# Value products scheduled in blocks of six pairs instead of single pairs, in a fused bucketed-attention and MLP kernel

## The chip, the cores and the metric

The kernel runs on one core of a Trainium2 chip. The metric is the device time of one execution in microseconds, as the median of several runs. Inside the core, TensorE (PE in the profile), VectorE (DVE), ScalarE (ACT) and GpSimd (POOL) work in parallel, each on its own queue of instructions in a fixed order; SyncE (SP) issues nearly all DMAs. An instruction that has to wait holds up everything behind it on its engine.

## What is computed

The reference is an attention layer in which a query sees only the keys of its own hash bucket, followed by a two-layer MLP with a squared ReLU. The sizes are 4 batches, 8 heads, 768 positions, head width 64, model width 512 and hidden width 2048:

```python
q_bits = (np.einsum('bhsd,dk->bhsk', q, proj) > 0)      # 6 bits, likewise k_bits
mask = q_bucket[:, :, :, None] == k_bucket[:, :, None, :]
scores = np.where(mask, scale * np.matmul(q, k.transpose(0, 1, 3, 2)), -1000000000.0)
attn = np.exp(scores - np.max(scores, axis=-1, keepdims=True))
attn = attn / (np.sum(attn, axis=-1, keepdims=True) + 1e-09)
x = np.matmul(attn, v)                                  # heads side by side: 3072 x 512
h = np.maximum(x @ w_in, 0.0)
out = h * h @ w_out
```

## The kernel before

**Work.** The attention is cut into 32 visits: a batch, a pair of heads and a half of the queries (384 of 768). A visit has six units, one for each head and each block of 128 queries. A unit (`unit`, line 669) multiplies queries and keys into the tile `pS` on PE, finds the row maximum `nmx` on DVE, takes the exponential `e` with its sum `sm` on ACT, and divides by the sum. In most visits the result is split into a high and a low float16 part, `hl`, which a DMA transposes into `aT`. In five early visits (`PLAIN_AV`, line 54) it stays float32 and PE transposes it through `pT`.

**Value products.** When the six units of a visit are done, `av` (line 707) multiplies `aT` by the values and accumulates in the PSUM tile `pA`. The two heads of the pair lie side by side: each matmul is 128 rows by 64 columns of TensorE, one head writes partitions 0 to 63 and the other 64 to 127, and the two of a pair run at the same time. A split visit takes 18 such pairs (six key chunks for each of high times high, low times high and high times low; values `VV`), a plain visit six pairs in float32 (values `V`). `xx`, the result in two float16 parts, is the input of the MLP.

**MLP.** When the four visits of a half batch are done, `moe` (line 726) computes the hidden layer into `pm` (384 columns in a matmul) and the output into `po` (512 columns), both with all 128 rows and columns of TensorE. There are eight such stages. They are the work that fills TensorE while softmax is under way; `pace` and `PACE` (lines 801 and 62) hold their matmuls back until given units have begun.

**What sets the order.** The functions do not issue instructions. They record operations in a `Program`, with their dependences and a rank. `order` (line 236) then plays the program through with assumed durations, backward for priorities and forward for an order on every engine, `ROUNDS` (4) times, and keeps the shortest plan. In `forward` (line 309) an engine that comes free takes the ready operation of the best priority. What it takes, it takes whole: an operation named `matmuls` holds a list of matmuls, which `emit` (line 392) issues one behind the other. Line 370 adds `SWITCH` (95 ns assumed) where an operation on PE uses another tiling than the one before it (`tiling`, line 219: rows and columns, so 128 by 64 for the value products, 128 by 128 for scores and MLP). The recorded order is issued as it stands, and nothing is reordered at run time.

Before the change each pair of value matmuls is one such operation:

```python
for n, (kc, d0, c) in enumerate(todo):
    matmuls(*[(pA[m], VV[:, h, kc, d0 : d0 + D], aTs[h][:, c]) for h, m in enumerate((T, U))],
            start=n == 0, stop=n == len(todo) - 1)
```

So between any two pairs of a visit the planner may put another operation: a score matmul, an MLP matmul, or a bucket matmul (`pc`).

Of the kernel before, what the change touches and what calls it, by code (L numbers as in the profile page):

```python
# [24 lines left out]
B, H, S, D = 4, 8, 768, 64  # L25
# [26 lines left out]
PLAIN, PLAIN_TO, ALTERNATE = 4, 8, 36  # L52

PLAIN_AV, DIVIDE = (0, 1, 2, 4, 5), ("pool",)

WHOLE = {0: 2}

# [373 lines left out]
def lsh_attention_moe(ctx: ExitStack, tc, kq, v, proj2, w_in, w_out, consts, out):  # L431
# [4 lines left out]
    pr = Program(tc)  # L436
    pe, dve, act, pool, sp = pr.pe, pr.dve, pr.act, pr.pool, pr.sp
    T, U = slice(0, D), slice(D, P)
# [6 lines left out]
    def move(out, x, scale=1.0, engines=(act, dve, pool)):  # L445
        ways = [(q, "tensor_scalar", (out, x, scale, 1.0, ALU.mult, ALU.mult), {}) for q in engines if q not in (act, sp)]
        if act in engines:
            ways.append((act, "activation", (out, x, AF.Identity if isinstance(scale, View) else AF.Copy), {"scale": scale}))
        if sp in engines:
            ways.append((sp, "dma_start", (out if out.dtype == x.dtype else out.bitcast(x.dtype), x), {}))  # L450
        pr.add(*ways)

    def left(out, x, scale, part):
        ways = [(dve, "scalar_tensor_tensor", (out, x, scale, part, ALU.mult, ALU.subtract), {})]
        if not isinstance(scale, View) and scale == 1.0:
            ways.append((pool, "tensor_tensor", (out, x, part, ALU.subtract), {}))
        pr.add(*ways)

    def sb(shape, dtype, name, bufs=1, tag=None):
        return pr.tile(sbp, "sb", shape, dtype, name, BUFS.get(tag or name, bufs), tag)  # L460

    def ps(shape, dtype, name, bufs=1, tag=None):
        return pr.tile(psp, "psum", shape, dtype, name, bufs, tag)
# [113 lines left out]
    def matmuls(*args, start=True, stop=True):  # L577
        pr.add((pe, "matmuls", [(a, {"start": start, "stop": stop}) for a in args], {}))
# [128 lines left out]
    def av(b, hp, half, VV, aTs):  # L707
        pA = ps([P, 512], F32, "pA")[:, 0:HS]
        plain = VV.dtype == F32
        todo = [(kc, t * D, kc + l * KC) for t, l in (((0, 0),) if plain else ((0, 0), (1, 0), (0, 1))) for kc in range(KC)]  # L710
        scale = vscales[b][0] if plain else 1.0 / ASC
        for n, (kc, d0, c) in enumerate(todo):
            matmuls(*[(pA[m], VV[:, h, kc, d0 : d0 + D], aTs[h][:, c]) for h, m in enumerate((T, U))], start=n == 0, stop=n == len(todo) - 1)
        xx = xxs[b, half, hp] = sb([P, 2, HS], F16, "xx")
        move(xx[:, 0], pA, scale)
        left(xx[:, 1], pA, scale, xx[:, 0])
# [117 lines left out]
    for n, (b, hp, half) in enumerate(visits):  # L834
        sts, aTs, plain = kept[b, hp], [], n in PLAIN_AV
        for h, st in enumerate(sts):
            aT = sb([P, KC, HS], F32, "aT") if plain else sb([P, 2 * KC, HS], F16, "aT")
            aTs.append(aT)
            for i in range(3):
                pr.rank = u  # L840
                unit(st, half, i, aT, plain)
                u += 1
        if n + 1 < len(visits):
            ready(*visits[n + 1][:2], u + PREP, n + 1 < PLAIN_TO and visits[n + 1][1] < PLAIN)
        if (b, hp, plain) not in kept_v or not alive([kept_v[b, hp, plain]]):
            pr.rank = u - 6 + PREP
            kept_v[b, hp, plain] = values(b, hp, plain)
        pr.rank = u - 0.5
        av(b, hp, half, kept_v[b, hp, plain], aTs)
        if n in early:  # L850
            do, j, pr.rank = early[n]
            do(j)
        done[b, half] = done.get((b, half), 0) + 1
        if done[b, half] == H // 2:
            moe(stages, b, half)
            stages += 1
# [35 lines left out]
```

## Time and profile before

| what | value |
|---|---|
| time, median of 3 runs | 905.26 us (904.71 to 906.72) |
| span of the profiled execution | 905.9 us |
| PE busy | 875.5 us, 97% |
| DVE busy | 614.0 us, 68% |
| ACT busy | 638.4 us, 70% |
| POOL busy | 108.5 us, 12% |
| mean granted TensorE clock | 0.998 |
| matmuls / weight loads recorded | 5090 / 5090 |

The span of 905.9 us runs from the first to the last instruction of the profiled execution; the page gives no other time for that execution, and the median of the timed runs lies 0.64 us below it. Busy time of PE is the union of the recorded matmuls, whose ends are modelled and overlap the next one's start. What a matmul takes from PE is therefore read from start to start, not from its recorded duration. In a timeline a row merges equal neighbours: its first two numbers are the start of the first and the time to the end of the last. All functions record through one helper, so nearly every row has the line L418 (L415 for a list of matmuls); the tile names tell the rows apart. A float32 matmul is recorded as two.

### The profile page before, as it was taken

Reading aid. Unit: us, or ns where it says so; the run is one execution under the profiler, and the core shown is the slowest. Engines: PE = TensorE matmul, PEld = TensorE weight load, DVE = VectorE, ACT = ScalarE, POOL = GpSimd, SP = SyncE. Lnnn points to the kernel's source line nnn. Section 1 sums busy time; section 2 is a strip of 40 time slices with the busy share of each in tenths; the row PEclk is TensorE's granted clock in tenths of the full one; section 3 lists DMA queues with packets and bytes.
Section 4 is the critical chain, followed back from the end, with each engine's and each line's share of the span. In section 5 each row is a group of like instructions: output and inputs, shape, how many; then the busy total and the mean of one; then the engine's idle time right before and its main releaser. Section 6 shows DMA issues by size and latency. Waiting matters only on the chain. (4 is left out here: it accounts for less than half of the span.)

```text
span 905.9 us, 14199 instructions
## 1 busy us (share of the span) xinstructions
PE 875.5 (97%) x5090; PEld 478.0 (53%) x5090; DVE 614.0 (68%) x1154; ACT 638.4 (70%) x1175; POOL 108.5 (12%) x159
## 2 busy tenths in 40 slices
PE   7998999999999999999999999999999999999997
PEld 5553544455555555555555555555555555544553
DVE  5899989978887778787776868886867651211111
ACT  3887676969797787888876877877767663432433
POOL 1665655100100000000000000000000000000000
PEclk9999999999999999999999999999999999999999
DMA  7548649978969797979897969896979452200000
GB/s 230 161 145 191 179 142 230 198 138 174 187 146 210 152 208 147 221 145 216 153 210 142 192 133 204 177 197 124 194 128 193 90 101 32 57 1 1 35 1 35
DMA packets 279974, 131.82 MB, mean 146 GB/s; under 512 B 258272, under 2 KB 258400, under 8 KB 279904
## 3 DMA queue, kind: packets, MB, share of 16 engines
q1 hardware_dynamic: 279424, 130.91, 68.9%
q8 instruction: 40, 0.66, 0.3%
q14 instruction: 30, 0.25, 0.1%
q10 hardware_dynamic: 480, 0.01, 0.0%
HBM read 37.30 MB, written 6.29 MB: 48 GB/s over the span
## 5 line engine op out<-in xcount | busy, mean ns | idle before, releaser
L418 PE MATMUL po<-wo,g 128*128 128x512 f16 x1152 | 334.3, 380 | 1.1 <-ACT o L418 0.8
L418 PE MATMUL pm<-xx,win 128*128 128x384 f16 x1536 | 322.6, 327 | 1.8 <-ACT xx L418 1.5
L418 DVE TENSOR_REDUCE nmx<-pS 128x1 f32<-128x768 f32 x192 | 182.9, 953 | 64.1 <-PE pS L418 61.2
L418 ACT ACTIVATE e<-pS,nmx 128x768 f32<-128x768 f32 x192 | 171.8, 895 | 70.1 <-DVE nmx L418 61.6
L418 PEld LDWEIGHTS <-win 128*128 128x128 f16 x1536 | 145.3, 98 | 114.7 <-issue 16.7
L418 DVE SCALAR_TENSOR_TENSOR hl<-e,rv,hl 128x768 f16<-128x768 f32 x162 | 164.0, 1013 | 20.9 <-ACT hl L418 20.5
L418 PEld LDWEIGHTS <-g 128*128 128x128 f16 x1152 | 107.2, 98 | 128.4 <-issue 26.4
L418 ACT ACTIVATE hl<-e,rv 128x768 f16<-128x768 f32 x156 | 144.5, 930 | 26.8 <-ACT e L418 18.3
L418 DVE SCALAR_TENSOR_TENSOR g<-g,g 128x384 f16<-128x384 f32 x123 | 68.4, 557 | 130.3 <-ACT g L418 129.3
L418 ACT ACTIVATE g<-pm 128x384 f32<-128x384 f32 x127 | 61.7, 486 | 106.5 <-PE pm L418 105.3
L418 ACT ACTIVATE g<-g 128x384 f32<-128x384 f32 (+1 forms) x252 | 130.8, 521 | 5.2 <-PE po L418 0.2
L415 PE MATMUL pA<-aT,VV 128*64 128x384 f16 x972 | 102.8, 332 | 0.0
L418 PE MATMUL pS<-A,Q 128*128 128x384 f32 x288 | 93.6, 405 | 5.9 <-ACT e L418 4.3
L418 POOL TENSOR_SCALAR rv<-sm 128x1 f32<-128x1 f32 x72 | 29.9, 415 | 528.1 <-ACT e L418 492.9
L418 PE MATMUL pS<-L,M 128*128 128x384 f32 x288 | 76.7, 346 | 2.5 <-DMA M<-Q 2.3
L415 PEld LDWEIGHTS <-VV 128*64 128x64 f16 x972 | 50.1, 109 | 50.4 <-issue 35.0
L418 PEld LDWEIGHTS pS<-A,Q 128*128 128x128 f32 x288 | 47.9, 189 | 34.5 <-ACT e L418 20.9
L418 PEld LDWEIGHTS pS<-L,M 128*128 128x128 f32 x288 | 51.4, 188 | 7.2 <-issue 3.5
L418 DVE TENSOR_SCALAR rv<-sm 128x1 f32<-128x1 f32 x120 | 18.2, 152 | 36.3 <-ACT e L418 33.1
L418 PE MATMUL pS<-A,L 128*128 128x384 f32 x96 | 38.4, 517 | 4.1 <-ACT e L418 3.6
L418 DVE TENSOR_SCALAR M<-pc,cst 128x384 fp32r<-128x384 f32 (+1 forms) x56 | 37.5, 670 | 1.8 <-PE pc L418 1.6
L418 PE MATMUL pS<-Q,M 128*128 128x384 f32 x96 | 37.3, 501 | 1.4 <-ACT e L418 1.4
(111 smaller groups left out, 671.1 us busy)
## 6 DMA issues: line engine op xcount, KB each, us to landing
R<-kq SPq DMA_DIRECT2D x24, 384.0 KB, 4.1
raw<-w_in SPq DMA_DIRECT2D x16, 511.8 KB, 3.5
raw<-w_out SPq DMA_DIRECT2D x16, 511.8 KB, 4.5
V<-vp SPq DMA_DIRECT2D x16, 384.0 KB, 4.9
out<-o SPq DMA_DIRECT2D x21, 256.0 KB, 3.5
Q<-L SPq DMA_DIRECT2D x24, 192.0 KB, 3.7
Q<-A SPq DMA_DIRECT2D x24, 192.0 KB, 3.1
A<-A SPq DMA_DIRECT2D x24, 192.0 KB, 3.5
```

The source lines that it names most:

```text
L415: ins = q.engine.matmul(*map(real, args), **kw).ins
L418: ins = getattr(q.engine, o.name)(*map(real, o.args), **{k: real(x) for k, x in o.kw.items()}).ins
```

## The change

`av` collects the matmuls of the pairs in a list and hands the list over after every sixth pair. A split visit becomes three operations of six pairs (twelve matmuls) instead of 18 of one pair, and a plain visit one operation of six pairs instead of six. The matmuls themselves, their operands and their order within the visit are the same.

```diff
+AV_RUN = 6
...
+        run = []
         for n, (kc, d0, c) in enumerate(todo):
-            matmuls(*[(pA[m], VV[:, h, kc, d0 : d0 + D], aTs[h][:, c]) for h, m in enumerate((T, U))], start=n == 0, stop=n == len(todo) - 1)
+            run += [((pA[m], VV[:, h, kc, d0 : d0 + D], aTs[h][:, c]), {"start": n == 0, "stop": n == len(todo) - 1}) for h, m in enumerate((T, U))]
+            if (n + 1) % (AV_RUN if not plain else 6) == 0:
+                pr.add((pe, "matmuls", run, {}))
+                run = []
```

The planner lays out the whole program anew with these larger operations, so the order changes on every engine. Three places show how. The first is the order of PE in the last attention visit, where only MLP output (`po`) and value products (`pA`) are left to choose from. Before:

```order
L418 LDWEIGHTS g_9290
L418 MATMUL po_8880<-wo_805,g_9290 128x512
L415 LDWEIGHTS VV_6961
L415 MATMUL pA_9122<-aT_8510,VV_6961 64x384
L415 LDWEIGHTS VV_6961
L415 MATMUL pA_9122<-aT_8821,VV_6961 64x384
L418 LDWEIGHTS g_9290
L418 MATMUL po_8880<-wo_805,g_9290 128x512
L415 LDWEIGHTS VV_6961
L415 MATMUL pA_9122<-aT_8510,VV_6961 64x384
```

After, the end of one block of the same visit:

```order
L417 LDWEIGHTS VV_6842
L417 MATMUL pA_9283<-aT_8484,VV_6842 64x384
L417 LDWEIGHTS VV_6842
L417 MATMUL pA_9283<-aT_8813,VV_6842 64x384
L417 LDWEIGHTS VV_6842
L417 MATMUL pA_9283<-aT_8484,VV_6842 64x384
L417 LDWEIGHTS VV_6842
L417 MATMUL pA_9283<-aT_8813,VV_6842 64x384
L420 LDWEIGHTS g_9297
L420 MATMUL po_8872<-wo_882,g_9297 128x512
```

A single pair between two `po` matmuls has become the end of a run of six pairs. The second place is on PE in the visit whose value tile is `pA_5853` in both orders, in the middle of the program, where a group of score matmuls (`pS`, two rows of two matmuls) meets the value products. Before:

```order
L415 LDWEIGHTS VV_4559
L415 MATMUL pA_5853<-aT_5698,VV_4559 64x384
L418 LDWEIGHTS sgn_157
L418 MATMUL pc_5919<-bits_5708,sgn_157 128x384
L418 MATMUL pS_5924<-A_5405,Q_5447 128x384 x2
L418 MATMUL pS_5924<-L_5419,M_5430 128x384 x2
L415 LDWEIGHTS VV_4559
L415 MATMUL pA_5853<-aT_5544,VV_4559 64x384
```

After:

```order
L417 LDWEIGHTS VV_4610
L417 MATMUL pA_5853<-aT_5511,VV_4610 64x384
L417 LDWEIGHTS VV_4610
L417 MATMUL pA_5853<-aT_5699,VV_4610 64x384
L420 MATMUL pS_5874<-A_5354,Q_5377 128x384 x2
L420 MATMUL pS_5874<-L_5375,M_5386 128x384 x2
L417 LDWEIGHTS VV_4610
L417 MATMUL pA_5853<-aT_5511,VV_4610 64x384
```

Scores still break into this visit's value products, but only between blocks: the visit's 36 matmuls stand in four runs (4, 24, 6 and 2) before and in two (12 and 24) after. The third place is the start of SP's queue, with the first loads. Before:

```order
L418 DMA A<-kq 128x768
L418 DMA Q<-kq 128x768
L418 DMA R<-kq 64x768 x2
L418 DMA sgn_f<-consts 6x64 x4
L418 DMA V<-vp 128x768 x4
L418 DMA raw<-w_in 128x2047 x2
```

After:

```order
L420 DMA Q<-kq 128x768
L420 DMA A<-kq 128x768
L420 DMA sgn_f<-consts 6x64 x4
L420 DMA R<-kq 64x768 x2
L420 DMA V<-vp 128x768
L420 DMA raw<-w_in 128x2047 x2
L420 DMA V<-vp 128x768 x3
```

The constants `sgn_f` have moved ahead of the queries `R`, and the first weights `raw` ahead of three of the four value loads. Counted through the whole order of PE, the value products stand in 136 runs before (124 of `VV`, 12 of `V`) and in 71 after (66 and 5).

## Prediction

> **What bounds the kernel now.** I read the page first: its span, the busy times and the chain that ended last.
>
> ```profile
> span 905.9 us, 14199 instructions
> PE 875.5 (97%) x5090; PEld 478.0 (53%) x5090; DVE 614.0 (68%) x1154; ACT 638.4 (70%) x1175; POOL 108.5 (12%) x159
> PE 42%; DMA 1%; ACT 1%; DVE 0%; SPq 0%; issue 0%
> ```
>
> PE is busy nearly throughout and is the only engine with a share worth naming in the chain. The windows then tell where (columns: stretch, its length, busy time of PE, PEld, DVE, ACT, POOL, clock, DMA share, GB/s):
>
> ```profile
> 0.00:150.00 150.00, 135.78 (x740) 76.09 (x741) 128.06 (x264) 103.86 (x208) 81.26 (x111) 0.99 0.66 183
> 150.00:700.00 550.00, 540.02 (x3261) 298.63 (x3260) 432.74 (x794) 439.86 (x788) 27.19 (x48) 1.00 0.89 175
> 700.00:850.00 150.00, 149.09 (x824) 76.97 (x823) 44.44 (x82) 74.01 (x141) 0.00 (x0) 1.00 0.24 50
> ```
>
> Up to 150 us PE and DVE are both loaded (91% and 85%) and PE is not alone in setting the pace. From 150 to 700 us PE is at 98%, DVE at 79%, ACT at 80%. Behind that PE is alone. What PE loses to waiting after 150 us stands in the groups of that stretch (last numbers: idle time ahead of the group):
>
> ```profile
> L418 PE MATMUL po<-wo,g 128*128 128x512 f16 x1152 | 334.3, 380 | 1.1 <-ACT o L418 0.8 <-POOL g L418 0.4
> L418 PE MATMUL pm<-xx,win 128*128 128x384 f16 x1512 | 318.3, 327 | 1.1 <-ACT xx L418 0.9
> L418 PE MATMUL pS<-A,Q 128*128 128x384 f32 x288 | 93.6, 405 | 5.9 <-ACT e L418 4.3 <-DMA A<-A 1.4
> L418 PE MATMUL pS<-L,M 128*128 128x384 f32 x288 | 76.7, 346 | 2.5 <-DMA M<-Q 2.3
> L418 PE MATMUL pS<-A,L 128*128 128x384 f32 x12 | 4.6, 506 | 0.5 <-ACT e L418 0.5
> ```
>
> That is 11.1 us in 756, most of it ahead of scores. So after 150 us the time is the sum of what PE's instructions cost it, and a busy PE may still be a slow PE: the recorded durations overlap, and the cost must be read from start to start.
>
> **The price of a run of value products.** This is PE's timeline in the middle (start, time to the last end, count):
>
> ```profile
> 450.45 0.99 PE L418 MATMUL pm<-xx,win 128*128 128x384 f16 x5
> 451.27 1.24 PE L418 MATMUL po<-wo,g 128*128 128x512 f16 x5
> 452.44 0.68 PE L415 MATMUL pA<-aT,VV 128*64 128x384 f16 x6
> 453.05 0.62 PE L418 MATMUL pS<-A,Q 128*128 128x384 f32 x2
> 453.51 0.51 PE L418 MATMUL pS<-L,M 128*128 128x384 f32 x2
> 453.94 2.14 PE L415 MATMUL pA<-aT,VV 128*64 128x384 f16 x24
> 456.02 0.34 PE L418 MATMUL pc<-bits,sgn 128*128 128x384 bf16 x1
> ```
>
> Pitch first. Five `pm` start in 0.82 us, 0.164 each, and going over to `po` costs nothing. The five `po` span 1.24 us, the last of them 0.38 (the group's mean), so four pitches are 0.86 and one is 0.215. The run of 12 pairs holds PE for 2.08 us (453.94 to 456.02) and the run of 3 for 0.61 (452.44 to 453.05): nine pairs more cost 1.47 us, 0.163 a pair. A pair thus costs what one `pm` costs, and its weight loads are hidden. The rest is paid once a run. Going in: five `po` at 0.215 end at 452.35 and the first pair starts at 452.44, 0.09 us late. Inside and going out: 0.61 less three pairs is 0.12, and 2.08 less twelve is 0.12. A run costs 0.21 us whatever its length.
>
> The tail shows the same on the shortest runs, in the chain of waits (start, time on the chain):
>
> ```profile
> 804.38 0.22 PE po L418
> 804.59 0.28 PE pA L415 x2
> 804.88 0.32 PE po L418
> ```
>
> One pair and one `po` take 0.28 + 0.32 = 0.60 us where their pitches make 0.163 + 0.215 = 0.38: 0.22 us again. I take 0.215.
>
> The Trainium skill has the cause: "TensorEngine Tiling (Array Packing)", section Key Properties, says that changing the tiling mode drains the TensorE, and the rows agree that there is a fixed price at each change. "TensorE: Matmul & The Clock Gate", section Step-by-step, puts a drain at about 128 cycles; at the page's 2.4 GHz that is an estimate of 53 ns a change, 0.107 us a run, and 65 runs fewer would then give 7.0 us and a time near 899. The trace has both changes at nearly twice that, so the trace's price is used.
>
> **The change part by part.** *Fewer runs of split values.* The order has 66 runs of `VV` instead of 124, 58 fewer, all in the stretch where PE sets the pace (ahead of the first MLP matmul both orders have one run, of 18 pairs). 58 times 0.215 is 12.5 us (12.2 at 0.21, 12.8 at 0.22). The matmuls are the same, so nothing is added on PE.
>
> *Fewer runs of plain values.* Seven runs of `V` fewer, all in the first 150 us. Their price:
>
> ```profile
> 36.52 1.51 PE L415 MATMUL pA<-aT,V 128*64 128x384 f32 x8
> 37.96 0.34 PE L418 MATMUL pc<-bits,sgn 128*128 128x384 bf16 x1
> 38.23 1.51 PE L415 MATMUL pA<-aT,V 128*64 128x384 f32 x8
> ```
>
> From the single `pc` at 37.96 to the next run is 0.27 us, of which 0.163 is its pitch: 0.11 going in, about what a split run pays, so I use the same 0.21 a run, 1.5 us in all. PE does not set the pace alone there; I count half, 0.7 us, with 0 and 1.5 as ends.
>
> *A new start.* SP's first loads change places:
>
> ```profile
> 1.65 5.59 SPq L418 DMA_DIRECT2D R<-kq  x2
> 7.36 1.45 SPq L418 DMA_DIRECT2D sgn_f<-consts  x4
> 10.32 0.43 DVE L418 CAST sgn<-sgn_f 128x512 bf16<-128x512 f32 x1 [7.65 <-DMA sgn_f<-consts]
> ```
>
> `sgn_f` now goes ahead of `R`, so that cast can come earlier by up to the 5.59 us that the `R` issues take; but `R`, which the first scores need as well, comes 1.45 us later. Ends -1.5 and +1.5 us, value 0. Up to the first MLP matmul both orders have the same 40 units begun, so no stage has moved across the border.
>
> *New waits.* A score group that becomes ready just behind the start of a block now waits for up to six pairs, 6 times 0.163 = 0.98 us, instead of one; behind it on PE stand the rest of the block and MLP matmuls, and on the other side `nmx`, `e` and the transposes wait for it. Whether PE then pays is a question of slack in the softmax loop:
>
> ```profile
> 501.00 0.95 DVE L418 TENSOR_REDUCE nmx<-pS 128x1 f32<-128x768 f32 x1
> 501.98 0.90 ACT L418 ACTIVATE e<-pS,nmx 128x768 f32<-128x768 f32 x1 [0.57 <-DVE nmx L418]
> 503.13 0.65 PE L418 MATMUL pS<-A,Q 128*128 128x384 f32 x2
> 504.17 0.96 DVE L418 TENSOR_REDUCE nmx<-pS 128x1 f32<-128x768 f32 x1 [0.56 <-PE pS L418]
> 150.00:780.00 630.00, 143.10 (x150) 147.71 (x300) 1.00 0.83 163
> 771.04 0.47 PE L418 MATMUL pS<-L,M 128*128 128x384 f32 x1
> ```
>
> One turn of the loop, from maximum to maximum, takes 3.17 us. The last two rows give the turns to be made: 150 maxima (the tile `nmx` in that window) until the last score at 771 us, 621 us for 150, 4.14 us each. So a turn has 0.97 us to spare on average, just what a block costs at worst, and meanwhile PE works on the block. Against the 11.1 us of waiting now I put +1 us, with -4 (a third of it goes) and +8 (three quarters more) as ends, since the new order is another draw and no row fixes it.
>
> **The sum.** From the profiled execution: 905.9 - 12.5 - 0.7 + 0 + 1.0 = 893.7 us. The median lies 0.64 us under that span, so 893.1 us. Low end: 12.8, 1.5 and 4 all at their best give 905.26 - 18.3 = 887. High end: 12.2, 0 and +8 give 901.
>
> **The rivals.** *Slower: scores stuck behind blocks.* In the new order 29 score groups stand directly behind a value run (28 before). If each came a whole block late and PE stood still for it afterwards, that is 29 times 0.98 = 28 us against 13.2 gained: 905.26 - 13.2 + 28 = 920. It decides at 0.46 us for each, just under half a block. For it: the loop's rows show ACT and DVE waiting for each other and for `pS` in turn, with one score tile in use. Against it: the slack of 0.97 us a turn, and a ready stock of MLP matmuls, with which PE waited so little for `e`. I give it 0.05.
>
> *No change: PE is not what sets the pace between 150 and 700 us.* Then the time saved there turns into waits for softmax, and only runs behind the last score count: 11 in the order before, 6 after, 5 times 0.215 = 1.1 us, a time of 904.2. The Trainium skill speaks for it: "Perfetto Trace Analysis", section Identifying the Most-Contended Engine, warns that matmul busy time is no good measure of a TensorE near its limit. The trace bears out that recorded matmuls overlap (0.38 us recorded, 0.215 apart). Against the rival is what the pitches show: between 450 and 456 us nothing is open but the fixed prices of runs and of score groups. 0.05.
>
> *Half eaten.* The mechanism holds but waits grow by more than 8 us, without passing what decides for no change: 901 to 903.4 us, say 902.5. The new order is laid out by assumed durations, and nothing holds its waits to those of the old. 0.06. On the other side, waits that fall by more than 4 us (say to half, 887 less 1.5, 885.5) have 0.02.
>
> **How the numbers follow.** The forecast, with its bounds, has 0.82, and its time is 893.1. The range is its own, 887 to 901; the other cases outside it hold 0.18. About 0.2%, 1.8 us, is what a measurement of this kernel can tell from no change, so up to 903.4 counts as faster: 0.82 + 0.06 + 0.02 = 0.90 faster, 0.05 the same, 0.05 slower.
>
> **What would show it.** Right: pairs still 0.163 us apart, each run still about 0.21 us dear, 71 runs, MLP tail without single pairs, PE's idle time after 150 us near 12 us, the span shorter by about the number of runs gone times their price. Wrong in the slower way: idle time ahead of `pS` of 20 us and more with ACT `e` or DVE `nmx` as its end. Wrong in the other: PE's busy time falls by 13 us and its idle time rises by as much between 150 and 700 us. A first MLP matmul that starts over 2 us away from where it started before would show that the new start was underrated.

## The result, and the profile after

The changed kernel takes 893.75 us in the median of four runs (892.07 to 897.11), the kernel before beside it 905.87 us. The ratio is 0.9863 with a 95% interval of 0.9835 to 0.9890: faster by 12.1 us, 1.4%. The forecast was 893.1 us, in a range of 887 to 901.

The profiled execution of the changed kernel is the slowest of its four runs: 897.11 us, with a span of 895.3 us against 905.9 before. Its page:

```profile
span 895.3 us, 14201 instructions
PE 860.8 (96%) x5082; PEld 478.9 (53%) x5082; DVE 612.0 (68%) x1149; ACT 641.3 (72%) x1180; POOL 110.5 (12%) x159
PE 46%; DMA 2%; ACT 2%; DVE 2%; issue 1%; SPq 0%; ACTq 0%
```

PE's busy time has fallen by 14.7 us; no other engine's has changed by more than 3. The windows, cut as before:

```profile
0.00:150.00 150.00, 130.85 (x709) 74.02 (x710) 123.11 (x256) 106.54 (x213) 76.11 (x106) 0.95 0.64 179
150.00:700.00 550.00, 541.22 (x3313) 304.83 (x3312) 438.88 (x805) 444.45 (x796) 34.38 (x53) 1.00 0.90 177
700.00:850.00 150.00, 148.75 (x851) 79.37 (x850) 42.46 (x78) 74.30 (x142) 0.00 (x0) 1.00 0.22 46
```

Between 150 and 700 us PE gets 3313 matmuls done in place of 3261, with the same busy share. In the first 150 us it has done 31 fewer, at a mean clock of 0.95 (below). The waits after 150 us, by group:

```profile
L420 PE MATMUL po<-wo,g 128*128 128x512 f16 x1152 | 330.0, 380 | 0.9 <-ACT o L420 0.8
L420 PE MATMUL pm<-xx,win 128*128 128x384 f16 x1532 | 328.9, 327 | 1.8 <-ACT g L420 1.6
L420 PE MATMUL pS<-A,Q 128*128 128x384 f32 x288 | 93.1, 403 | 5.7 <-ACT e L420 5.7
L420 PE MATMUL pS<-L,M 128*128 128x384 f32 x288 | 76.5, 346 | 1.6 <-DMA M<-Q 1.6
```

They make 10.0 us, 11.1 before. The middle of the program, in PE's timeline, shows the visit `pA_5853` of the order (12 and 24 matmuls):

```profile
496.00 1.17 PE L417 MATMUL pA<-aT,VV 128*64 128x384 f16 x12
497.09 0.62 PE L420 MATMUL pS<-A,Q 128*128 128x384 f32 x2
497.55 0.52 PE L420 MATMUL pS<-L,M 128*128 128x384 f32 x2
497.99 2.14 PE L417 MATMUL pA<-aT,VV 128*64 128x384 f16 x24
500.06 0.50 PE L420 MATMUL pm<-xx,win 128*128 128x384 f16 x2
```

The run of 12 pairs still holds PE for 2.07 us (497.99 to 500.06), the run of six for 1.09: six pairs more cost 0.98, or 0.163 each, as before. The cleanest price stands at the end, behind the last score. The timeline gives that score and the chain of waits the value products after it:

```profile
763.86 0.47 PE L420 MATMUL pS<-L,M 128*128 128x384 f32 x1
```

```profile
820.77 0.22 PE po L420
820.99 1.10 PE pA L417 x12
822.09 0.32 PE po L420
822.41 1.10 PE pA L417 x12
823.50 0.32 PE po L420
823.83 1.10 PE pA L417 x12
```

Both kernels have the same work behind that score: 360 `pm`, 288 `po` and 18 pairs of `pA`. The pairs stand in 18 runs of one before and in these 3 runs of six after. From the start of that score to the end of the span it takes 134.9 us before (771.04 to 905.9) and 131.4 after (763.86 to 895.3): 15 runs fewer, 3.4 us, 0.23 us a run.

So the 10.6 us between the two profiled executions divide into 3.4 us behind the last score and 7.2 us ahead of it.

### The profile page after: what moved, and what is told of

Read it like the earlier page. It is cut to its first block, busy times and chain, and to the rows that moved or that the text cites. A ratio compares the mean times of both kernels' runs of the same rounds, so it can differ in the third digit from the quotient of the medians.

```text
span 895.3 us, 14201 instructions
## 1 busy us (share of the span) xinstructions
PE 860.8 (96%) x5082; PEld 478.9 (53%) x5082; DVE 612.0 (68%) x1149; ACT 641.3 (72%) x1180; POOL 110.5 (12%) x159
## 4 chain that ended last, share of the span: by engine, by line
PE 46%; DMA 2%; ACT 2%; DVE 2%; issue 1%; SPq 0%; ACTq 0%
PE po L420 18%; PE pm L420 17%; PE pS L420 6%; PE pA L417 5%; DMA M<-Q 1%; ACT o L420 1%; DVE nmx L420 1%; ACT g L420 1%; ACT hl L420 0%; DMA L<-M 0%; DMA Q<-L 0%; PE pd L417 0%; DVE hl L420 0%; ACT e L420 0%; PE pc L420 0%
## 5 line engine op out<-in xcount | busy, mean ns | idle before, releaser
L420 PE MATMUL pm<-xx,win 128*128 128x384 f16 x1536 | 330.2, 328 | 1.8 <-ACT g L420 1.6
L420 PE MATMUL po<-wo,g 128*128 128x512 f16 x1152 | 330.0, 380 | 0.9 <-ACT o L420 0.8
L420 ACT ACTIVATE hl<-e,rv 128x768 f16<-128x768 f32 x157 | 145.3, 929 | 24.3 <-ACT e L420 12.1
L420 ACT ACTIVATE g<-g 128x384 f16<-128x384 f32 (+1 forms) x251 | 130.4, 520 | 5.7 <-PE po L420 0.6
L417 PE MATMUL pA<-aT,VV 128*64 128x384 f16 x972 | 91.6, 329 | 0.0
L420 POOL TENSOR_SCALAR rv<-sm 128x1 f32<-128x1 f32 x71 | 27.3, 384 | 482.1 <-ACT e L420 480.3
L420 PE MATMUL pS<-Q,M 128*128 128x384 f32 x96 | 39.3, 526 | 4.6 <-ACT e L420 4.6
```

Of the source, the lines that this page charges most:

```text
L417: ins = q.engine.matmul(*map(real, args), **kw).ins
L420: ins = getattr(q.engine, o.name)(*map(real, o.args), **{k: real(x) for k, x in o.kw.items()}).ins
```

## The experiments

The theory was that a run of value products costs PE 0.215 us beside its pairs, so that the time follows the number of runs (price). Its rivals: the gain belongs to the new plan as such, which could as well have come out worse (layout, luck); scores wait behind blocks (waiting); and, formed after the first runs, in a plan that is laid out the MLP work between two score groups is fixed, so that PE time saved comes back as waits (fixed fill).

**The runs removed, the old plan kept.** When PE's instructions are written out, the pairs are held back until six are there. Nothing else moves.

```diff
+    def gather(self, out):
+        held, done = {}, []
+        for i in out:
...
+            held.setdefault(visit, []).append(i)
+            if len(held[visit]) == 6:
+                done += held.pop(visit)
```

> The kernel before, with the plan of before kept on every engine; only when PE's instructions are written out are the pairs of a visit held back to the place of the sixth pair, so that six stand together. 65 runs of value products instead of 136, nothing planned anew. Price theory (each run costs PE about 0.215 us): 71 fewer runs take 15 us off, 890 to 893 us. Layout theory (the gain of the changed kernel comes from its new plan, not from the runs): within 3 us of before, 903 to 908 us. Waiting theory (blocks hold up scores): the same 15 us, less what PE's idle time ahead of pS grows, so over 895 us with that idle time above 15 us.

Measured: 908.56 us against 906.75, ratio 1.0022 (1.0006 to 1.0038). With 71 runs fewer nothing is gained, within 3 us of before as the layout theory had it. The time has gone into waits. The weight loads of the scores, from 150 to 700 us, show it (waited in total, times, longest); before, then this kernel:

```profile
PEld pS L418 <- ACT e L418: 20.9, 56, 1.9
```

```profile
PEld pS L433 <- ACT e L433: 32.7, 76, 1.6
```

The score loads wait 11.8 us more for the exponential to leave the score tile. A count from start to start agrees: if each step between two matmuls after 150 us is taken less the usual step between matmuls of the same tiles in these traces, PE waits an estimated 15 us more than in the kernel before, as much as the runs were to give. Behind the last score, from 775.97 us to the end of the span at 909.2, the same three runs of six save 1.7 us, half of what they save in the changed kernel; a wait of 0.6 us for `g` stands there that the kernel before does not have. The price theory in the form "PE alone sets the pace" falls here; of the waiting theory's two conditions, over 895 us was met, and the recorded idle time ahead of `pS` after 150 us rose from 8.9 to 13.1 us, not over 15. This kernel cannot tell blocks that hold up scores from a fill that is fixed.

**The runs put back, the new plan kept.** The reverse, in the changed kernel: the first two blocks of a visit are cut up as they are written out.

```diff
+                    if len(args) == 12 and not held and not args[-1][1]["stop"]:
+                        held = [args[n : n + 2] for n in range(2, 12, 2)]
+                        args = args[:2]
...
+            if held and o.name == "matmul" and o.args[0].shape[1] >= HS and "is_transpose" not in o.kw and o.args[1].dtype == F16:
+                pairs(held.pop(0))
```

> The changed kernel with its new plan on every engine; only when PE's instructions are written out are the first and second block of a visit cut into single pairs, one after each following MLP matmul. 138 runs of value products instead of 71. Price theory: 67 more runs add 14 us to the changed kernel, 906 to 909 us, about the time before. Layout theory: the new plan keeps its gain, 893 to 897 us.

Measured: 913.52 us, ratio 1.0070 (1.0048 to 1.0091) to the kernel before, so some 19 us above the changed kernel for 67 runs more. The price accounts for 14.4. Here the time that is added to PE in a fixed plan is paid in full; what makes up the other 4 to 5 us was not isolated, since splitting a block also puts off its pairs behind later MLP matmuls. The time that was taken away in the kernel before is not given back.

**PE time removed without any block.** To part the two, 64 matmuls of the first layer are dropped in each of the two kernels as they are written out; plan and runs stay.

```diff
+                    if n in (1, 2, 3, 4) and cc == 2:
+                        pr.left_out.add(len(pr.ops))
                     pe.matmul(pm[:, 0:HS], wl, X[cc][:, 0], start=False, stop=cc == 0)
...
+            if i in self.left_out:
+                continue
```

> The kernel before, plan kept on every engine, value products in single pairs; 64 of the first layer's matmuls (in stages 1 to 4, one low-part product of twelve in each hidden tile) are left out as PE's instructions are written out, 64 times 0.163 = 10.4 us of PE time, all of it while softmax is under way. Price theory (PE alone sets the pace): 895 to 897 us. Fixed-fill theory (in a plan that is laid out already, the MLP work between two score groups is fixed, and PE time that is saved turns into waits ahead of the next scores): over 901 us, with PE's idle time ahead of pS up by 5 us or more.

> The changed kernel, plan kept on every engine, with the same 64 matmuls (10.4 us of PE time) left out. Price theory: 883 to 886 us. Fixed-fill theory: over 888 us, with PE's idle time ahead of pS up by 5 us or more.

Measured: 902.04 us for the kernel before (ratio 0.9956, 0.9939 to 0.9972), 892.42 for the changed one (0.9835, 0.9815 to 0.9854). Of the 10.4 us that PE no longer works, the one gets back about 4 us, the other, by the two ratios, 2.5, where the intervals of the two ratios overlap. Waits of the score loads have grown again; the old plan thinned:

```profile
PEld pS L421 <- ACT e L421: 31.2, 83, 2.0
```

The changed kernel, then the same thinned:

```profile
PEld pS L420 <- ACT e L420: 20.1, 53, 2.0
```

```profile
PEld pS L423 <- ACT e L423: 28.3, 71, 2.0
```

No value product has moved here, so these waits are not made by blocks: it is shown that in a plan which is laid out already a good part of the PE time saved does not come back (some 6 and 8 of the 10.4 us by the ratios) and that waits grow in its place. The fixed-fill theory's own sign, idle time ahead of `pS` up by 5 us, failed for the old plan as the groups count it (8.4 us after 150 us, 8.9 before). It held for the new one (12.3 against 7.3), but most of that rise is not softmax: the scores wait for a DMA there, 5.6 us against 1.6. The changed kernel thinned:

```profile
L423 PE MATMUL pS<-A,Q 128*128 128x384 f32 x288 | 92.4, 401 | 6.6 <-ACT e L423 6.2
L423 PE MATMUL pS<-L,M 128*128 128x384 f32 x288 | 76.6, 346 | 5.7 <-DMA M<-Q 5.6
```

Neither count is exact. The groups count a wait only from a matmul's modelled end, so too little. The rows of the weight loads count too much, because a load can wait while PE still works on the matmul ahead of it: in the old plan they grew by 10.3 us, yet the profiled execution is 7.2 us shorter (898.7 against 905.9). From start to start, as above, the waits grew by an estimate of 4 us in the old plan and 8 in the new.

**Longer blocks.** One constant, `AV_RUN = 18` and `AV_RUN = 9`, planned anew.

> The changed kernel with AV_RUN = 18: a split visit is one operation of 18 pairs, 32 runs instead of 71. Price theory: 39 fewer runs take another 8.4 us off, 884 to 887 us. Waiting theory: an operation now holds PE for 2.9 us against 0.97 us of slack in a turn of the softmax loop, PE's idle time after 150 us rises from 10 us by 8 us or more and the time is 893 us or above.

> The changed kernel with AV_RUN = 9: two operations of nine pairs a visit, 51 runs instead of 71. Price theory: 20 fewer runs take 4.3 us off, 888 to 891 us. Waiting theory: blocks of 1.5 us exceed the slack of 0.97 us, the gain of the fewer runs is eaten, 893 to 897 us.

Measured: 906.99 us for 18 (ratio 0.9994, 0.9981 to 1.0007) and 899.09 for nine (0.9906, 0.9884 to 0.9927), 2 us above even what the waiting theory gave. With 32 runs the whole gain is gone. For 18, three rows of the groups after 150 us:

```profile
L420 PE MATMUL po<-wo,g 128*128 128x512 f16 x1151 | 315.6, 381 | 3.5 <-DVE g L420 1.3 <-ACT o L420 1.0 <-DVE acc L420 0.8
L420 PE MATMUL pm<-xx,win 128*128 128x384 f16 x1512 | 314.2, 328 | 6.1 <-ACT g L420 2.6 <-DVE g L420 2.0 <-ACT xx L420 1.0
L420 PE MATMUL pS<-A,Q 128*128 128x384 f32 x288 | 93.1, 404 | 9.3 <-ACT e L420 8.7
```

Idle time after 150 us is 20.9 us in all (10.0 in the changed kernel, 16.3 with blocks of nine), and the score loads wait for `e` 33.0 us in 75 waits against 20.1 in 53. Both figures of the waiting theory were met at 18. Its mechanism is shown in part: of the 10.9 us more of idle time 2.0 stand ahead of scores (9.3 against 7.3), 4.3 ahead of `pm` and 2.6 ahead of `po`, by the groups. For `pm` these are mostly waits for `g`, which takes the hidden layer's result out of `pm`.

**Shorter blocks.** `AV_RUN = 3`.

> The changed kernel with AV_RUN = 3: blocks of 0.49 us, 93 runs instead of 71. Price with replanning: 22 more runs cost 4.7 us, 895 to 902 us. Luck theory: anywhere from 890 to 910 us. If waits behind blocks already matter at six pairs, PE's idle time between 150 and 700 us falls by 3 us or more and the time is 894 us or under.

Measured: 903.03 us, ratio 0.9958 (0.9943 to 0.9973), 1 us above the end that the price theory gave. Idle time from 150 us to the end is 11.7 us. That is not under the 10.0 of the changed kernel, so the waiting theory's figure failed; it is under the 13.8 to 16.2 of the other three plans with blocks of six (table below), so some waiting may begin there, which is not shown.

**Each part alone.** First plain visits as one operation with split visits in single pairs (`AV_RUN = 1`), then the other way round:

```diff
-            if (n + 1) % (AV_RUN if not plain else 6) == 0:
+            if (n + 1) % (AV_RUN if not plain else 1) == 0:
```

> One part of the change alone: plain visits as one operation of six pairs, split visits in single pairs (AV_RUN = 1). 134 runs, 129 of split values and 5 of plain ones. Price theory: two runs fewer than before, 903 to 908 us, so that all of the change's gain belongs to the split visits. Luck theory: a new plan, 8 us or more from before in either direction.

> The other part of the change alone: split visits in blocks of six pairs, plain visits in single pairs. 75 runs (65 of split values, 10 of plain ones). Price with replanning: the plain part was worth 1 us at most, 891 to 898 us. Luck theory: 901 us or above is as likely.

Measured: 908.22 us for the plain part (1.0014, 1.0001 to 1.0027), 900.01 us for the split part (0.9918, 0.9905 to 0.9931). Each is a fraction of a us to 2 us above what the price gave. The gain belongs to the split visits. That the two do not add up to 12 us has a reason that the last three runs show.

**The same kernels, planned anew.** One assumed duration is changed by less than one per cent.

```diff
-TRANSPOSES = 165
+TRANSPOSES = 166
```

> The kernel before with one assumed duration of the planner changed by less than one per cent (TRANSPOSES from 165 to 166): the same work, planned anew, 146 runs of value products instead of 136. Price theory: 10 more runs, 2.2 us, 906 to 910 us. Luck theory (each new plan is another draw, with waits that differ by as much as the change gained): 8 us or more from before, in either direction.

> The changed kernel with the planner's TRANSPOSES at 166 instead of 165: the same blocks, planned anew, 64 runs of value products instead of 71. Price with replanning (a run costs 0.215 us, a planner that knows of the blocks gets it back, and a new plan scatters by some 3 us): 889 to 896 us. Luck theory (the changed kernel's plan was a good draw): 901 us or above.

> As the last, with TRANSPOSES at 164: 66 runs. Price with replanning: 889 to 896 us. Luck theory: 901 us or above.

Measured: 912.22 us for the kernel before (1.0063, 1.0042 to 1.0083), 900.06 and 893.61 us for the changed one (0.9917, 0.9897 to 0.9936, and 0.9851, 0.9833 to 0.9870). A plan is a draw: four plans with blocks of six (the changed kernel, the two redraws and the split part alone) lie 7.1 to 13.6 us under the kernel before, three with single pairs (before, its redraw, the plain part) 0 to 5.4 us over it. The means are 10.0 under and 2.3 over, 12.3 us apart, for 69 and 139 runs on average: 0.18 us a run, or four fifths of the price. With plans that scatter by 3 us either way, this cannot be told from the whole price. Two of the three redraws lie outside what the price allowed, by 2 us (the kernel before) and 4 us. The luck theory's figure for the changed kernel, above 901 us, did not turn up; its core, that part of the 12.1 us is the draw, did: the changed kernel and the second redraw are good draws by 2 to 4 us.

All together, against the kernel before measured beside each:

| kernel | runs of value products | difference, us | idle PE after 150 us, us |
|---|---|---|---|
| before, TRANSPOSES 166 | 146 | +5.4 | 11.6 |
| before | 136 | 0 | 11.1 |
| plain part alone | 134 | +1.4 | 12.9 |
| blocks of 3 | 93 | -4.2 | 11.7 |
| split part alone | 75 | -7.2 | 16.2 |
| changed, blocks of 6 | 71 | -12.1 | 10.0 |
| changed, TRANSPOSES 164 | 66 | -13.6 | 13.8 |
| changed, TRANSPOSES 166 | 64 | -7.1 | 14.3 |
| blocks of 9 | 51 | -7.7 | 16.3 |
| blocks of 18 | 32 | +0.2 | 20.9 |
| old plan, pairs gathered | 65 | +1.8 | 17.1 |
| new plan, blocks cut | 138 | +6.8 | 12.9 |

The idle time is the sum over all groups of matmuls, from the one profiled execution of each kernel. Waits are not all that scatters: the redraw of the kernel before ran at mean clocks of 0.990 to 0.993 in its six executions, the kernel before beside it at 0.995 to 0.998. About 0.004 of 912 us is 4 us, an estimate, so most of its 5.4 us can be clock; its idle time is only 0.5 us higher. No kernel here beats the changed one by more than the runs can tell.

## Why the prediction was right, point by point

*The price of a run*, 0.215 us, is right: 15 runs less behind the last score saved 3.4 us, 0.23 each. By a bare drain, the estimate from the Trainium skill ("TensorE: Matmul & The Clock Gate", Step-by-step), they would have saved 1.6, so the measurement decides.

*The count*, 65 runs fewer, of them 58 with 12.5 us in the split visits, holds as a mean over plans: where the planner knew the blocks, the time follows the runs, down to blocks of six, at 0.18 us a run. That this one plan came within 0.7 us of the forecast is in part luck: the mean of the four plans with blocks of six lies 10.0 us under the kernel before, 2.1 us less than the changed kernel.

*What bounds the kernel* was too simple. The sentence "after 150 us the time is the sum of what PE's instructions cost it" is true behind the last score, and ahead of it only for a plan that is laid out with those costs. With the plan kept, a saving of 15 us (pairs gathered) gave nothing and one of 10.4 us a quarter to two fifths. Softmax and PE set the pace together there. Fewer runs in the old plan gained nothing, new plans without blocks gained nothing, and new plans with blocks of six gained 10.0 us in the mean: the forecast came out because the change goes through the planner, which is a reason that the prediction did not give. That such a planner brings the scores and the fill into step again is the likely reading; just what it moves to get the time back, the runs do not isolate.

*New waits*, +1 us with ends at -4 and +8, were -1.1 us by the same rows, and the bounds were needed: redraws of the same kernel have 3.8 and 4.3 us more idle time than the changed kernel.

*The start* was put at 0 us for the loads (ends 1.5 either way) and at 0.7 us gained by the plain runs. At its high end the range left out the 1.5 us of the loads, and at its low end 1.5 us stands once for two terms. The first MLP matmul starts at 139.10 us (row further down) instead of 140.90, 1.8 us earlier. Before:

```profile
140.90 0.32 PE L418 MATMUL pm<-xx,win 128*128 128x384 f16 x1 [0.68 <-ACT xx L418]
```

The loads and the cast after the change:

```profile
1.66 4.50 SPq L420 DMA_DIRECT2D sgn_f<-consts  x4
6.19 1.20 SPq L420 DMA_DIRECT2D R<-kq  x2
7.58 0.43 DVE L420 CAST sgn<-sgn_f 128x512 bf16<-128x512 f32 x1 [4.92 <-DMA sgn_f<-consts]
```

The cast comes 2.74 us earlier and the first score starts at 12.75 instead of 14.64 us. Not all of this is the order: in the kernel with the pairs gathered, which has the order of before, the two `R` take 4.74 us instead of 5.59. In this execution the lead is gone by 150 us, where PE has done 5 `pm` against 24 before; the half clock from 141 us on, below, falls into that stretch.

*The rivals.* Slower through scores behind blocks did not happen at six pairs; at 18 waits took the whole gain, though by the groups more of the added idle time stands ahead of MLP matmuls than of scores. "Half eaten", 901 to 903.4 us, was near: two of the four plans with blocks of six came out at 900. The rival "no change" had its mechanism half right, since saved time does turn to waits if the plan is kept; and its own figure was wrong, because the runs behind the last score were miscounted in the order (11 and 6, where the trace has 18 and 3): 15 runs times 0.215 are 3.2 us, so it would have given 902.0 us, not 904.2.

## What to carry to other kernels

Read what an engine pays for a change of form from start to start, at a place where the same work stands in long runs and in short ones, and multiply it by a count taken from the order. Time taken off one engine was given back here where that engine alone set the pace, or where the order was laid out anew with the new cost; in a fixed order most of it was lost to waits for the others. And where a planner makes the order, plan the same kernel two or three times with a negligible difference before a gain of 1% is put down to an edit: here such draws differed by up to 6.5 us.

## What the runs showed of the hardware

The clock of PE fell to half for whole stretches, which the busy shares hardly show. PE alone, changed kernel, then before (columns: stretch, length, PE busy, clock, DMA share, GB/s):

```profile
83.00:91.00 8.00, 5.82 (x17) 0.57 1.11 211
91.00:141.00 50.00, 44.25 (x235) 1.00 0.56 163
141.00:152.00 11.00, 8.90 (x19) 0.54 1.00 270
```

```profile
86.00:90.00 4.00, 3.33 (x6) 0.58 1.28 168
141.00:152.00 11.00, 10.11 (x46) 1.00 1.03 261
```

In the 11 us from 141 us on PE does 19 matmuls, nearly all at half clock, where it did 46 before. They follow a wait of 2.03 us for `e` behind the first MLP matmul, where the kernel before waits 0.56; that the wait lowered the clock is not shown:

```profile
139.10 0.33 PE L420 MATMUL pm<-xx,win 128*128 128x384 f16 x1
141.45 2.50 PE L420 MATMUL pS<-Q,M 128*128 128x384 f32 x4 [2.03 <-ACT e L420]
```

In the four runs of the changed kernel the span goes with the mean clock: spans of 890.3, 891.0, 892.8 and 895.3 us at mean clocks of 0.998, 0.996, 0.992 and 0.989. The profiled one is the slowest, 5.0 us behind the fastest, so some of the gain is missing from its trace. Whether a busier start would keep the clock up was not tried.

SP's queue pauses near its start, in every run behind its third DMA. The changed kernel with `TRANSPOSES` at 166 shows it between two rows:

```profile
1.65 0.58 SPq L420 DMA_DIRECT2D R<-kq  x1
5.89 1.34 SPq L420 DMA_DIRECT2D sgn_f<-consts  x4
```

Where the third DMA and the next ones are merged into one row, the pause lies inside it: the two `R` take 5.59 us when they stand there and 1.20 when they do not, the four `sgn_f` 4.50 and 1.45. It is not always one pause. In the kernel before, the second `R` starts at 6.76 us, 4.5 us behind the end of the first. In the changed kernel, the second `sgn_f` starts at 3.95 us, 1.9 us behind the first, and the third at 5.54, 1.3 us behind the second. In these two kernels the first scores start 1.89 us earlier with `sgn_f` in the third place.
